# Blockwise causal attention followed by a maxout MLP on one core: the loads and pieces of the opening stage in another order

## The chip, the core and the metric

The kernel runs on one core of one Trainium2 chip. The metric is the device time of one execution in microseconds, as the median of several runs. Engines are named as in the profile: PE (TensorE matmul), PEld (its weight loads), DVE (VectorE), ACT (ScalarE), POOL (GpSimd) and SP (SyncE, which here only issues transfers).

## The reference

Attention over 8 batches of 8 heads, 576 rows, head dimension 64, with a causal mask by blocks of 64; its output, laid out as 4608 tokens by 512, goes through an MLP whose hidden layer is the larger of two products. All inputs and the output are float32.

```python
scores = (1 / sqrt(64)) * q @ k.T              # per batch and head, 576 x 576
scores = where(row // 64 >= col // 64, scores, -1e9)
attn = softmax(scores) @ v
x = attn.transpose(0, 2, 1, 3).reshape(4608, 512)
h1, h2 = x @ w1, x @ w2                        # w1, w2: 512 x 1024
out = maximum(h1, h2) @ w_out                  # w_out: 1024 x 512
```

## The kernel before

**Work and units.** Two heads make a pair (32 pairs, four in each batch), two pairs a group (16 groups, numbered from 0; group g holds pairs 2g and 2g+1; groups 0 and 1 are batch 0, groups 2 and 3 batch 1). The MLP is rewritten with max(h1, h2) = h2 + max(h1 - h2, 0): `diff_w(j)` (line 183, on DVE) forms block j of `d_sb` = w1 - w2 out of the float32 block `w1raw` and the bfloat16 block of w2; there are four blocks of 256 columns. `m_unit` (line 249) forms `m_sb` = w2 @ w_out once. Then `h_unit(i, f)` (line 226) is four matmuls of 128x512 and a max with 0 on DVE (line 231), for the span i of 512 tokens and the slice f of 128 hidden columns: f = 0, 1 need block 0 of `d_sb`, f = 2, 3 block 1, f = 4, 5 block 2, f = 6, 7 block 3. `y_unit` (line 268) is twelve matmuls, a copy (273) and a store (274) for 128 tokens.

**The order is written out by hand.** There is no scheduler: each engine does its instructions in the order in which the program states them. MLP units stand in one list, and `fill(n)` puts the next n matmuls of that list (a matmul of `m_unit` counts a half) between pieces of attention, as far as the tokens they need are finished (`done_tokens`). So PE always has something in the program between two pieces of attention, but what it has there is fixed when the program is written.

**Attention of a group.** `load_qk(g, ..., gated=True)` puts a one-element memset of the raw buffer on POOL (line 114) and then a request for 576 KB of q and one for 576 KB of k on SP's queue (line 115); the memset holds SP back until POOL has come to that place. `cast` (155) turns the float32 rows into bfloat16, `transposes` (357) are 18 small matmuls for q and 18 for k, each into two PSUM buffers, which are copied out (365) by the two engines named in the call. `tile_0`, `tile_1`, `tile_2` compute scores (376, 394), ACT takes their exponential (400, 458), POOL zeroes the masked corners (`mask`, 405) and pads keys (`pad_keys`, 383). `av` (486) multiplies with V and normalizes on DVE (492, 493). `x_out` (524 to 530) transposes a group's result into `xT`, which frees tokens for the MLP; from group 4 on a transfer does this.

**Buffers and queues that matter here.** `ps_m` has four PSUM buffers in rotation; the outputs of `m_unit`, `h_unit`, `y_unit`, `transposes`, `av` and `x_out` all use them, so a matmul that begins a new buffer waits until the buffer's former content was read. `ps_s` has two, for scores. Requests for q and k go through SP's queue; those for V (`load_v`, five chunks for each batch), for w1 (`load_w1`, four blocks of 512 KB), w2 and w_out through POOL's, in the order of POOL's program.

**The opening stage.** Groups 0 and 1 (pairs 0 to 3) are written out call by call, then groups 2 and 3 of batch 1 up to the loop `for g in range(GPB + 1, NG)` (GPB = 2). In the loop, group g's first two score tiles come first, then for each of its pairs p a `fill`, `av_with(p - LAG, ...)` for the pair two before, the next group's `transposes`, two score tiles, and `pool_work(p)`, which issues the loads and casts of later groups. `pool_work(4)` and `pool_work(5)` are called ahead of the loop.

Of the kernel before, what the change touches and what calls it, by code (L numbers as in the profile page):

```python
# [14 lines left out]
def kernel(  # L15
# [91 lines left out]
    def load_qk(g, queues, gated=False):  # L107
        b, u = divmod(g, GPB)
        for nm, src, queue in (("q", q, queues[0]), ("k", k, queues[1])):
            if queue is None or by_dma(nm, g):  # L110
                continue
            raws[nm, g] = t = raw.tile([P, 2, RPP * D], FP32, name=f"{nm}raw")
            if gated:
                nc.gpsimd.memset(t[:, 0, :1], 0.0)
            queue.dma_start(
                out=t[:],
                in_=src[b, 4 * u:4 * u + 4].rearrange(
                    "(s h) (p t) d -> (h p) s (t d)", h=2, t=RPP),
            )
# [4 lines left out]
    def by_dma(nm, g):  # L124
        return g >= T_DMA.get(nm, NG)

    def load_blocks(nm, g):
        b, u = divmod(g, GPB)
        blk_n[nm, g] = n = raw.tile([P, S // BLK, 2, D], BF16, name=f"{nm}b", tag=f"{nm}raw")
        for h in range(2):  # L130
            for s in range(2):
                nc.gpsimd.dma_start(  # L132
                    out=n[h * BLK:(h + 1) * BLK, :, s],
                    in_=(q if nm == "q" else k)[b, 4 * u + 2 * s + h].rearrange(
                        "(j p) d -> p j d", p=BLK),
                )
# [10 lines left out]
    def cast(nm, g, parts):  # L147
        if by_dma(nm, g):
            return
        t = raws[nm, g].rearrange("p s (t d) -> p t s d", d=D)  # L150
        if (nm, g) not in qk_n:
            qk_n[nm, g] = qkn.tile([P, RPP, 2, D], BF16, name=f"{nm}n")
        n = qk_n[nm, g]
        for copy, j0, j1 in parts:
            copy(out=n[:, j0:j1], in_=t[:, j0:j1])  # L155

    def load_v(b, c):
        rows = min(P, S - c * P)
        nc.gpsimd.dma_start(  # L159
            out=vv_r[b % NV][P - rows:, c, :, :D],  # L160
            in_=v[b, :, c * P:c * P + rows, :].rearrange("h p d -> p h d"),
        )
# [12 lines left out]
    def load_w1(j):  # L175
        w1_raw[j] = wraw.tile([P, NDM, WB], FP32, name="w1raw")
        nc.gpsimd.dma_start(out=w1_raw[j][:], in_=w1r[:, :, j * WB:(j + 1) * WB])
# [149 lines left out]
    def fill(n):  # L327
        while n > 0:
            if not current:
                k = next((k for k, t in enumerate(todo) if t[2] <= done_tokens[0]), None)  # L330
                if k is None:
                    return max(0, n)
                current.append(todo.pop(k))
            t = current[0]
            next(t[1])
            n -= t[3]
            t[0] -= 1
            if not t[0]:
                current.pop()
        return 0  # L340
# [10 lines left out]
    def transposes(nm, g, copies):  # L351
        n = qk_n.pop((nm, g))
        pts = [ps_m.tile([P, RPP, NP], BF16, name=f"ps_{nm}T", tag="m") for _ in range(2)]
        for j in range(RPP):
            for i in range(2):
                r = slice(i * NP, (i + 1) * NP)
                nc.tensor.transpose(  # L357
                    pts[i][:, j, :], n[r, j].rearrange("p s d -> p (s d)"), ident[r, r],
                )

        def copy_out(which=(0, 1), part=(0, NP), copy=None):
            p0, p1 = part
            for i in which:
                t = (qT_r if nm == "q" else kT_r)[(2 * g + i) % NT]
                (copy or copies[i])(  # L365
                    out=t[:, p0 * RPP:p1 * RPP].rearrange("q (p j) -> q p j", j=RPP),
                    in_=pts[i][:, :, p0:p1].rearrange("q j p -> q p j"),
                )
        return copy_out
# [69 lines left out]
    def tile_0(p):  # L439
        u = ps_s.tile([P, 2, 512], FP32, name="ps_s", tag="s")  # L440
        scores(p, u, 0, 0, 0, 512)
        return lambda: (exp(p, u, 512, 0), mask(p, 0))

    def tile_1(p):
        u = ps_s.tile([P, 2, 512], FP32, name="ps_s", tag="s")
        scores(p, u, 0, 0, 512, 64)
        scores(p, u, 64, 1, 128, 448)
        return lambda: (exp(p, u, 512, 512), mask(p, 576))

    def tile_2(p):  # L450
        u = ps_s.tile([P, 2, 512], FP32, name="ps_s", tag="s")
        corner_scores(p, u, 320)
        scores(p, u, 0, 2, 256, 320)
        scores(p, u, 384, 3, 448, P)

        def out():
            exp(p, u, 512, 1024)
            nc.scalar.activation(  # L458
                out=aT_r[p % NA][BLK:, :, 1536:AW], in_=u[BLK:, :, 320:320 + BLK],
                func=AF.Exp, scale=scale,  # L460
            )
            mask(p, 1024)
            mask(p, 1344)
        return out

    def region(*tiles):
        for out in tiles:
            out()
# [29 lines left out]
    def x_by_dma(g):  # L498
        return BY_DMA <= g < NG - 1
# [47 lines left out]

    def pool_work(s):
        g, i = divmod(s, 2)
        if s == 4:  # L550
            load_qk(4, (SP, SP), gated=True)
        elif s == 5:
            load_qk(5, (SP, SP), gated=True)
            cast("q", 4, ((pool, 0, RPP),))
            cast("k", 4, ((pool, 0, RPP),))
        else:
            if i == 1 and g + 3 < NG:
                load_qk(g + 3, (SP, SP), gated=True)
            if i == 1 and g + 2 < NG:
                cast("q", g + 2, ((pool, 0, RPP),))  # L560
                cast("k", g + 2, ((pool, 0, RPP),))
            nb, j = divmod(s + 2, HP)
            if nb < B:
                for c in ((0, 1), (2, 3), (4,), ())[j]:
                    load_v(nb, c)
            for nm in "qk":
                if i == 1 and g + 3 < NG and by_dma(nm, g + 3):
                    load_blocks(nm, g + 3)

    T_AT = {s: [("qk"[s % 2], s // 2 + 1)] for s in range(NPAIR - 2)}  # L570
    T_AT[0] = T_AT[1] = T_AT[2] = T_AT[3] = []
# [62 lines left out]
    burst_q3(2)  # L634
    masks_q(2)
    load_w1(1)
    load_w1(2)
    fill(2)
    burst_q1(3)
    fill(2)  # L640
# [2 lines left out]
    av(2, [2, 3, 4])  # L643
    burst_q3(3)
    masks_q(3)
    load_w1(3)
    cast("q", 2, ((pool, 0, RPP),))
    load_qk(3, (SP, SP), gated=True)
    cast("k", 2, ((pool, 0, RPP),))
    load_v(1, 0)  # L650
    fill(8)
    av(3, [2, 3, 4])
    fill(4)
    x_out(1, 0, NCH, (act, act))
    fill(4)
    transposes("q", 2, (dve, act))()
    transposes("k", 2, (dve, act))()
    pad_keys(4)
    pad_keys(5)
# [1 line left out]
    diff_w(0)  # L661
    fill(4)
    region(tile_0(4), tile_1(4))
    load_v(1, 2)
    load_v(1, 3)
    fill(8)
    region(tile_2(4), tile_0(5))
    load_v(1, 4)
    diff_w(1)
    fill(8)  # L670
    region(tile_1(5), tile_2(5))
    diff_w(2)
    cast("q", 3, ((pool, 0, RPP),))
    cast("k", 3, ((pool, 0, RPP),))
    fill(4)
    diff_w(3)
    n = fill_of(GPB)
    fill(n // 2)
    transposes("q", 3, (dve, act))()
    pool_work(4)  # L680
    fill(n // 3)
    transposes("k", 3, (dve, act))()
    pad_keys(6)
    pad_keys(7)
    pool_work(5)
    fill(n - n // 2 - n // 3)

    for g in range(GPB + 1, NG):
        a, b = 2 * g, 2 * g + 1
        old = done_tokens[0]  # L690
        if x_due:
            x_out(x_due.pop())
        n, new = fill_of(g), done_tokens[0]
        region(tile_0(a), tile_1(a))
        lo, hi = max(3, n // 18), n * 2 // 9
        for p, tiles in ((a, lambda: (tile_2(a), tile_0(b))), (b, lambda: (tile_1(b), tile_2(b)))):
            done_tokens[0] = old if p == a and x_by_dma(g - 2) else new
            fill(hi)
            av_with(p - LAG, lo)
            done_tokens[0] = new  # L700
            if p % 2 and x_by_dma(g - 1):
                x_dma(g - 1)
            if p % 2 == 0:
                for nm in "qk":
                    if g + 1 < NG and by_dma(nm, g + 1):
                        transpose_blocks(nm, g + 1)
            copy_out = t_pair(p)
            outs = tiles()
            copy_out()
            region(*outs)  # L710
            if p % 2 and g + 1 < NG:
                pad_keys(p + 1)
                pad_keys(p + 2)
            pool_work(p)
        x_due.append(g - 1)
        fill(n - 2 * (lo + hi))
    for p in range(NPAIR - LAG, NPAIR):
        if x_due:
            x_out(x_due.pop())
        av_with(p, 5)  # L720
        if p % 2 and x_by_dma(p // 2):
            x_dma(p // 2)
        fill(9)
# [42 lines left out]
```

## Time and profile before

| | us |
|---|---|
| median of 3 runs (258.1 to 258.43) | 258.12 |
| the profiled execution's own time | 258.55 |
| its span, first to last instruction | 256.8 |
| PE busy | 245.8 (96%) |
| DVE, ACT, POOL busy | 149.6, 119.6, 122.8 |
| mean granted TensorE clock | 0.997 |

The page lists each engine's busy time, 40 slices of the span, the chain of work that ended last, and groups of instructions; single answers of the trace (waits, timelines, transfers, busy time by stretch) are read for one part of the span. A time such as 28.92 is in microseconds from the first instruction. The end of a matmul is modelled, so PE's busy share says where it is idle, not how well it is used.

### The profile page before, as it was taken

To read this page: it belongs to the slowest core of one execution; us is meant where nothing else is said; L and a number is where in the kernel's file an instruction comes from. 1 tells how busy PE (TensorE), PEld (TensorE's weight loads), DVE (VectorE), ACT (ScalarE), POOL (GpSimd) and SP (SyncE) were. 2 spreads that over 40 slices of the span, in tenths; PEclk is the share of its full clock that TensorE was granted. 3 is DMA by queue.
4 is the path that set the end of the run, shared out by engine and by line. 5 is a ranking of instruction groups with operands and counts; after the bars stand their busy time and mean duration, and the time that the engine had idled before them with its cause. 6 is when DMAs were issued, how large, how long until landed. Compare 5 with 4: busy or idle time off the path is not lost.

```text
span 256.8 us, 6746 instructions
## 1 busy us (share of the span) xinstructions
PE 245.8 (96%) x2768; PEld 132.8 (52%) x2768; DVE 149.6 (58%) x300; ACT 119.6 (47%) x159; POOL 122.8 (48%) x289
## 2 busy tenths in 40 slices
PE   8899898988999999999999999999999999999994
PEld 2467553645555555555555555455545564444443
DVE  4987569557476457545753575357635754753521
ACT  2876492778555555556464646464646300000000
POOL 1984565589768556855675568547231100000000
PEclk9999999999999999999999999999999999999998
DMA  7999999889999999999999999999961312111222
GB/s 247 213 156 249 342 313 131 304 80 214 193 152 201 156 213 157 215 159 219 159 208 151 219 161 201 148 225 154 112 140 59 79 43 83 41 43 41 80 84 83
DMA packets 104383, 41.27 MB, mean 161 GB/s; under 512 B 89248, under 2 KB 93728, under 8 KB 104352
## 3 DMA queue, kind: packets, MB, share of 16 engines
q0 software_dynamic: 65952, 11.87, 61.6%
q1 hardware_dynamic: 37984, 28.32, 46.3%
q10 hardware_dynamic: 416, 0.66, 0.7%
q8 instruction: 21, 0.34, 0.6%
q14 instruction: 10, 0.08, 0.1%
HBM read 34.60 MB, written 9.44 MB: 172 GB/s over the span
## 4 chain that ended last, share of the span: by engine, by line
PE 81%; POOL 6%; DMA 6%; ACT 3%; issue 2%; DVE 1%; POOLq 0%
PE ps_y L268 34%; PE ps_h L226 23%; PE ps_o L486 9%; PE ps_s L376 7%; DMA wo_sb<-in_moe_w_out_dram 4%; PE ps_w L346 2%; DMA vv<-in_v_dram 2%; PE ps_qT L357 2%; ACT aT L400 2%; PE ps_M L249 2%; POOL kb L132 1%; POOL xT L180 1%; POOL qn L155 1%; PE ps_y L283 1%; POOL aT L405 1%
## 5 line engine op out<-in xcount | busy, mean ns | idle before, releaser
L400 ACT ACTIVATE aT<-ps_s 128x1024 bf16<-128x1024 f32 (+2 forms) x100 | 95.8, 994 | 43.7 <-PE ps_s L376 32.9
L268 PE MATMUL ps_y<-wo_sb,g 128*128 128x512 bf16 x280 | 71.1, 380 | 0.0
L226 PE MATMUL ps_h<-xT,d_sb 128*128 128x512 bf16 x288 | 67.9, 380 | 0.0
L231 DVE TENSOR_SCALAR g<-ps_h 128x512 bf16<-128x512 f32 x72 | 49.6, 690 | 19.0 <-PE ps_h L226 18.9
L405 POOL MEMSET aT<- 64x128 bf16 x128 | 23.1, 201 | 66.2 <-ACT aT L400 65.4
L273 DVE COPY y<-ps_y 128x512 f32<-128x512 f32 x35 | 24.2, 692 | 45.5 <-PE ps_y L268 44.7
L486 PEld LDWEIGHTS <-aT 128*128 128x128 bf16 x960 | 37.5, 98 | 14.6 <-issue 1.2
L226 PEld LDWEIGHTS <-d_sb 128*128 128x128 bf16 x288 | 26.5, 98 | 31.2 <-issue 2.6
L268 PEld LDWEIGHTS <-g 128*128 128x128 bf16 x280 | 24.7, 98 | 30.3 <-issue 5.7
L486 PE MATMUL ps_o<-vv,aT 128*128 128x65 bf16 x960 | 39.9, 194 | 0.4 <-DMA vv<-in_v_dram 0.4
L268 PE MATMUL ps_y<-m_sb,xT 128*128 128x512 bf16 x140 | 38.4, 379 | 0.0
L159 POOL DMA_DIRECT2D vv<-in_v_dram x40 | 34.0, 855 | 0.9 <-issue 0.5
L376 PE MATMUL ps_s<-qT,kT 64*128 64x128 bf16 (+6 forms) x344 | 31.6, 281 | 2.6 <-ACT aT L458 1.5
L493 DVE TENSOR_TENSOR xp<-ps_o,rec 128x256 bf16<-128x256 f32 (+1 forms) x64 | 31.4, 490 | 2.2
L132 POOL DMA_DIRECT2D kb<-in_k_dram x40 | 29.4, 760 | 0.0
L492 DVE RECIPROCAL rec<-ps_o 128x4 f32<-128x4 f32 (+1 forms) x64 | 11.9, 186 | 23.7 <-PE ps_o L486 23.4
L288 ACT COPY y<-ps_y 128x256 f32<-128x256 f32 (+1 forms) x2 | 0.6, 320 | 49.3 <-PE ps_y L283 49.3
L365 ACT COPY qT<-ps_qT 128x576 bf16<-128x576 bf16 x15 | 9.6, 640 | 26.9 <-PE ps_qT L357 26.9
L155 POOL CAST qn<-qraw 128x1152 bf16<-128x1152 f32 (+1 forms) x15 | 17.1, 1141 | 7.1 <-DMA qraw<-in_q_dram 6.0
L268 PEld LDWEIGHTS <-xT 128*128 128x128 bf16 x140 | 12.8, 98 | 13.5 <-issue 0.5
L376 PEld LDWEIGHTS <-kT 64*128 64x128 bf16 x344 | 11.8, 94 | 14.2 <-issue 9.0
L365 DVE COPY qT<-ps_qT 128x576 bf16<-128x576 bf16 x17 | 12.7, 749 | 0.7 <-PE ps_qT L357 0.7
(58 smaller groups left out, 135.7 us busy)
## 6 DMA issues: line engine op xcount, KB each, us to landing
qraw<-in_q_dram SPq DMA_DIRECT2D x16, 576.0 KB, 4.6
out_dram<-y SPq DMA_DIRECT2D x35, 256.0 KB, 3.4
vv<-in_v_dram POOLq DMA_DIRECT2D x32, 128.0 KB, 5.5
kraw<-in_k_dram SPq DMA_DIRECT2D x5, 576.0 KB, 7.6
kb<-in_k_dram POOLq DMA_DIRECT2D x40, 72.0 KB, 6.5
w1raw<-in_moe_w_dram POOLq DMA_DIRECT2D x4, 512.0 KB, 13.9
xT<-in_moe_w_dram POOLq DMA_DIRECT2D x4, 256.0 KB, 6.2
wo_sb<-in_moe_w_out_dram POOLq DMA_DIRECT2D x2, 512.0 KB, 10.9
```

Source lines behind the costliest of these rows:

```text
L132: nc.gpsimd.dma_start(out=n[h * BLK:(h + 1) * BLK, :, s], in_=(q if nm == "q" else k)[b, 4 * u + 2 * s + h].rearrange("(j p) d -> p j d", ...
L159: nc.gpsimd.dma_start(out=vv_r[b % NV][P - rows:, c, :, :D], in_=v[b, :, c * P:c * P + rows, :].rearrange("h p d -> p h d"),)
L226: nc.tensor.matmul(pt[:], d_sb[:, c, f * P:(f + 1) * P], xT[:, c, t0:t0 + SPAN], start=(c == 0), stop=(c == NDM - 1),)
L231: nc.vector.tensor_scalar_max(g[:, f], pt[:], 0.0)
L268: nc.tensor.matmul(py[:], lhs, rhs, start=(n == 0), stop=(n == len(terms) - 1),)
L273: nc.vector.tensor_copy(out=y[:], in_=py[:])
L365: (copy or copies[i])(out=t[:, p0 * RPP:p1 * RPP].rearrange("q (p j) -> q p j", j=RPP), in_=pts[i][:, :, p0:p1].rearrange("q j p -> q p j"),)
L376: nc.tensor.matmul(ps[:, hh, col:col + w], kT[r, k0:k0 + P], qT[r, q0:q0 + w], start=True, stop=True,)
L400: nc.scalar.activation(out=aT_r[p % NA][:, :, a0:a0 + w], in_=ps[:, :, :w], func=AF.Exp, scale=scale,)
L405: (eng or nc.gpsimd).memset(aT_r[p % NA][BLK:, :, a0:a0 + BLK], 0.0)
L486: nc.tensor.matmul(po[:, gi, hh, :], a[:, hh, a0:a0 + P], vv[:, c, h0 + 2 * hh, :], start=(mm == 0), stop=(mm == n_mm - 1),)
L493: nc.vector.tensor_mul(xp[:, :, ts[0]:ts[0] + n, p % 2].rearrange("q s t d -> q t s d"), po[:, :, :, :D], rec[:, :n].to_broadcast([P, n, 2 ...
```

## The change

In the opening stage the requests, casts and fillers stand elsewhere; in the loop group 3 and 4 differ. Nothing is computed differently, and PE has the same number of matmuls.

- Group 3's q and k are requested directly behind the masks of pair 3, ahead of group 2's casts. Blocks 2 and 3 of w1 are requested later, between chunks of V.
- q of group 3 is cast on POOL right after the first two score tiles of pair 4; k of group 3 is cast on DVE, behind `diff_w(1)`. The transposes of group 3 stand before and behind the last two score tiles of pair 5; those of k are copied out by DVE alone.
- Groups 4 and 5 are requested at earlier places of the program; their special cases in `pool_work` go.
- `diff_w(2)` and `diff_w(3)` come later relative to the hidden units, and there are fewer fillers ahead of the loop (28 matmuls of `h_unit` before, 17 after, ahead of the scores of pair 6).
- `av` of pairs 6 and 7 comes half a group sooner, and `x_out(3)` with it.

```diff
     def pool_work(s):
         g, i = divmod(s, 2)
-        if s == 4:
-            load_qk(4, (SP, SP), gated=True)
-        elif s == 5:
-            load_qk(5, (SP, SP), gated=True)
-            cast("q", 4, ((pool, 0, RPP),))
-            cast("k", 4, ((pool, 0, RPP),))
-        else:
-            if i == 1 and g + 3 < NG:
-                load_qk(g + 3, (SP, SP), gated=True)
...
+        if i == 1 and g + 3 < NG:
+            load_qk(g + 3, (SP, SP), gated=True)
...
     masks_q(2)
     load_w1(1)
-    load_w1(2)
     fill(2)
...
     masks_q(3)
-    load_w1(3)
+    load_qk(3, (SP, SP), gated=True)
     cast("q", 2, ((pool, 0, RPP),))
-    load_qk(3, (SP, SP), gated=True)
     cast("k", 2, ((pool, 0, RPP),))
     load_v(1, 0)
+    load_w1(2)
     fill(8)
     av(3, [2, 3, 4])
     fill(4)
     x_out(1, 0, NCH, (act, act))
     fill(4)
     transposes("q", 2, (dve, act))()
+    fill(5)
     transposes("k", 2, (dve, act))()
     pad_keys(4)
     pad_keys(5)
     load_v(1, 1)
     diff_w(0)
     fill(4)
     region(tile_0(4), tile_1(4))
+    cast("q", 3, ((pool, 0, RPP),))
     load_v(1, 2)
-    load_v(1, 3)
+    load_w1(3)
+    load_qk(4, (SP, SP), gated=True)
+    diff_w(1)
+    cast("k", 3, ((dve, 0, RPP),))
     fill(8)
     region(tile_2(4), tile_0(5))
+    load_v(1, 3)
     load_v(1, 4)
-    diff_w(1)
     fill(8)
-    region(tile_1(5), tile_2(5))
+    copy_out = transposes("q", 3, (dve, act))
+    outs = tile_1(5), tile_2(5)
+    copy_out()
+    region(*outs)
+    fill(4)
     diff_w(2)
-    cast("q", 3, ((pool, 0, RPP),))
-    cast("k", 3, ((pool, 0, RPP),))
-    fill(4)
-    diff_w(3)
-    n = fill_of(GPB)
-    fill(n // 2)
-    transposes("q", 3, (dve, act))()
-    pool_work(4)
-    fill(n // 3)
-    transposes("k", 3, (dve, act))()
+    transposes("k", 3, (dve, dve))()
     pad_keys(6)
     pad_keys(7)
-    pool_work(5)
-    fill(n - n // 2 - n // 3)
+    load_qk(5, (SP, SP), gated=True)
+    cast("q", 4, ((pool, 0, RPP),))
+    cast("k", 4, ((pool, 0, RPP),))
+    fill(4)

     for g in range(GPB + 1, NG):
...
+            if p == 6:
+                diff_w(3)
             fill(hi)
-            av_with(p - LAG, lo)
+            if p == 9:
+                x_out(3)
+                new = done_tokens[0]
+            else:
+                av_with(p - 1 if p == 8 else p - LAG, lo)
...
-        x_due.append(g - 1)
+        if g != GPB + 2:
+            x_due.append(g - 1)
         fill(n - 2 * (lo + hi))
+        if g == GPB + 1:
+            av_with(6, lo)
```

More of the change, by code (lines that the diff above doesn't have):

```diff
@@ L549, in pool_work @@
         g, i = divmod(s, 2)
-        if s == 4:
-            load_qk(4, (SP, SP), gated=True)
-        elif s == 5:
-            load_qk(5, (SP, SP), gated=True)
-            cast("q", 4, ((pool, 0, RPP),))
-            cast("k", 4, ((pool, 0, RPP),))
-        else:
-            if i == 1 and g + 3 < NG:
-                load_qk(g + 3, (SP, SP), gated=True)
[L559 to L568, printed above, removed]
+        if i == 1 and g + 3 < NG:
+            load_qk(g + 3, (SP, SP), gated=True)
+        if i == 1 and g + 2 < NG:
+            cast("q", g + 2, ((pool, 0, RPP),))
+            cast("k", g + 2, ((pool, 0, RPP),))
+        nb, j = divmod(s + 2, HP)
+        if nb < B:
+            for c in ((0, 1), (2, 3), (4,), ())[j]:
+                load_v(nb, c)
+        for nm in "qk":
+            if i == 1 and g + 3 < NG and by_dma(nm, g + 3):
+                load_blocks(nm, g + 3)
     T_AT = {s: [("qk"[s % 2], s // 2 + 1)] for s in range(NPAIR - 2)}
```

## The prediction

> **What bounds the kernel now.** I read the page's busy times and slices first, to see which engine fills the span and where it does not.
>
> ```profile
> PE 245.8 (96%) x2768; PEld 132.8 (52%) x2768; DVE 149.6 (58%) x300; ACT 119.6 (47%) x159; POOL 122.8 (48%) x289
> ...
> PE   8899898988999999999999999999999999999994
> ```
>
> PE bounds it. From the eleventh slice (70 us) on it is never idle until 252.9. The order of PE's program differs only between the transposes of group 2's k (about 29 us) and about 87 us; ahead of and behind that it is instruction for instruction the same, and the matmuls are the same in number. So the time can change only by PE's idle time in between. Second, the busy time of the stretch 28 to 70, and who made PE wait in it (columns: total, times, longest):
>
> ```profile
> 28.00:70.00 42.00, 37.84 (x567) 21.55 (x565) 26.72 (x49) 28.83 (x42) 30.45 (x66) 1.00 1.21 222
> ```
>
> ```profile
> PE ps_s L376 <- ACT aT L458: 1.5, 2, 0.8
> PE ps_kT L357 <- POOL kn L155: 1.2, 1, 1.2
> PE ps_qT L357 <- POOL qn L155: 0.8, 1, 0.8
> PE ps_o L486 <- DMA vv<-in_v_dram: 0.4, 1, 0.4
> ```
>
> The idle time is 42 - 37.84 = 4.16 us: the most that the change can bring (1.6%). Third, timelines of PE, POOL, SP and DVE, for the places:
>
> ```profile
> 30.12 0.44 PE L357 MATMUL ps_kT<-ident,kn 64*128 64x64 bf16 x18 [1.20 <-POOL kn L155]
> ...
> 41.13 0.44 PE L357 MATMUL ps_qT<-ident,qn 64*128 64x64 bf16 x18 [0.76 <-POOL qn L155]
> ...
> 44.42 0.61 PE L376 MATMUL ps_s<-qT,kT 64*128 64x512 bf16 x6
> ```
>
> ```profile
> 39.34 1.74 POOL L155 CAST qn<-qraw 128x1152 bf16<-128x1152 f32 x1
> ```
>
> ```profile
> 27.88 0.41 SPq L115 DMA_DIRECT2D kraw<-in_k_dram  x1
> ```
>
> ```profile
> 33.78 1.23 DVE L183 TENSOR_TENSOR d_sb<-w1raw,xT 128x1024 bf16<-128x1024 f32 x1 [0.66 <-DMA w1raw<-in_moe_w_dram]
> ```
>
> The row at 44.42 is the scores of pair 6; by then PE has done 28 matmuls of the hidden layer. Last, the transfers between 32 and 34 us (packets, MB, share of the engines):
>
> ```profile
> q0 software_dynamic: 120, 0.44, 61.1%
> q1 hardware_dynamic: 122, 0.28, 42.0%
> ```
>
> POOL's queue (q0) and SP's (q1) share the engines packet for packet; together they move 350 to 366 GB/s in the stretches from 28 to 36.
>
> [...] the q cast at 39.34 stood behind masks though q had landed at 36.9. [...] that cast took 1.74 us beside a subtraction on DVE, casts of the same size without it 1.14.
>
> **The requests.** The masks of pair 3 end at 24.0 on POOL, so k of group 3 is requested at about 24.6 instead of 27.88. Before, it landed 11.8 us after its request, at 39.7. From 28.0, when group 2's k is nearly in, the bytes ahead of its end were four blocks of w1 (2.10 MB), q and k (1.18) and a V chunk (0.13): 3.41 MB at 355 GB/s are 9.6 us, up to 37.6; the last part lagged 2.1 us. Now only two blocks of w1 come first: 2.36 MB, 6.6 us, and the same lag give **36.7** as an estimate (35.3 with two thirds of the lag gone, 37.6 if V's small packets hold it up). But block 1 of w1 now shares with q and k from the start: at 0.28 MB for every 0.44, its 1.05 MB take 4.8 us instead of some 3.6, so it lands at about 34.9 instead of 33.75; block 0 at 32.6 instead of 31.9.
>
> **PE up to q's transposes.** Ten m_unit matmuls (0.98 us for 8 in the chain of waits, so 1.2) fill the wait of 1.20 ahead of k's transposes. They need w_out's second half, which landed at 29.1 (16.42 + 12.7), so they start 0.2 late: gain 1.0. Block 0 of w1 (32.6 + 1.23) costs about 0.2 at the first hidden matmul. Fourteen m_unit matmuls, four score tiles and nine hidden matmuls later PE stands at the transposes of group 3's q at about 36.7.
>
> **The new wait.** The second buffer of these transposes is the one of the first hidden unit, so it needs that unit's max on DVE. In DVE's order the max stands behind diff_w(1) and **behind the cast of k that waits for k's landing**. Diff: 34.9 + 1.22 = 36.1. Cast: starts at 36.75, 1.34 us (group 1's k cast on DVE), 38.0. Max: 0.69 less overlap, 38.65. PE waits 36.7 to 38.7, **2.0 us**, where it waited 0.76. Queued on DVE behind the cast are two maxes, a q copy, diff_w(2), both k copies, diff_w(3). So, on PE: transposes 0.4 (39.1), two score tiles 0.7 (39.8), four hidden matmuls at 0.216 (40.65), k's transposes 0.4 (41.05), three hidden (41.7). The next needs block 2: its max chain (40.6 + 0.65) and diff_w(2) 1.22 end at 42.45, a wait of 0.75; pair 6's scores need the first k copy (0.7): **43.1**. That is 1.3 earlier than 44.42, but only 17 hidden matmuls are done, not 28; the other 11 cost 2.4 later. Break-even is 42.05, so PE is 1.05 us behind.
>
> **Behind that.** DVE still owes a k copy, two maxes and diff_w(3), up to about 46: waits of PE of 0.4 at an av and 0.4 at q's transposes of group 4. V's chunks 3 and 4 of batch 1 are now requested at about 38.3 and 39.2, behind block 3 of w1: they land at 43 with the 3.9 us of a quiet queue, at 47 with the 7.7 of a loaded one, and are needed at 46.5: 0 to 0.6, taken as 0. Of the old waits, the two on ACT (1.5) have about the same causes, with other fillers: 1.1 to 1.5; the V wait (0.44) can go, as batch 2's chunks stand further ahead. Waits behind 44.42 were 1.95 and become about 2.1: +0.15.
>
> **What costs nothing.** Earlier requests for groups 4 and 5 (37.7 instead of 42.23): their casts are not waited for long; covered by PE's fillers. Block 2 is needed at 41.2 and lands near 38.5; block 3, issued behind q's cast and a V chunk near 37, lands at 43 to 44.5 for 44.2 on DVE: 0 to 0.3. POOL loses a cast (1.14); its q cast now stands ahead of a V chunk (0.88 to issue), block 3 (0.75) and pair 4's last masks, up to 2 us late, but pair 4's av needs these only at 46. SP's requests and stores keep their order. Pairs 6 and 7 and x_out(3) half a group sooner change which filler runs on a PE that is never idle there.
>
> **Sum:** +1.05 + 0.15 = +1.2 us. The profiled execution took 258.55 (span 256.8 and 1.75 around it), so it would take 259.75; it stands 0.43 above the median, so against the median of 258.12: **259.3**.
>
> **Rivals.** 0.2%, or 0.5 us, is about what a measurement can tell from no change. (A) Faster: k lands before PE asks. If it is in and diff_w(1) done by 35.1, the wait falls from 2.0 to 0.5 and the sum is -0.3; with the 0.8 on DVE behind it half gone, -0.7: 257.4. For it: the requests are 3.3 us sooner, and the lag of 2.1 us may not return. Against: block 1 must then land as early as before, though it now shares. It decides at k's landing and block 1 both ahead of 35. (B) No change: k at 35.9, +0.3, 258.4: the old waits are exchanged for one on DVE of equal size. (C) Worse: k at 37.6 and V's last chunk after 47: +0.9 and +0.6, 260.8. That the moves do not take effect is no rival: each engine's program has them, with DVE's k cast ahead of the first max.
>
> **How the numbers follow.** The main case 0.55, C 0.15, B 0.17, A 0.13. Slower is the main case and C, 0.70; same B, 0.17; faster A, 0.13. The range goes from 257.7, inside A, to 260.7, just short of C's end, and leaves out some two tenths.
>
> **What would show it.** Right: PE ps_qT waits for DVE g (L231) about 2 us near 38.7; the cast of k on DVE begins when kraw lands, 36 to 37; PE's wait for POOL kn at 30 is gone; pair 6's scores at about 43. Wrong: kraw landed before 35.2 and no such wait (A); or a long wait of ps_o for vv near 47 (C); or PE idle behind 70 us, which no step here foresees.

## The result, and the profile after

The changed kernel takes **266.37 us** (median of 4 runs, 266.01 to 267.24) against 258.11 for the kernel before beside it (257.68 to 258.43): ratio **1.0326, 95% interval 1.0297 to 1.0355**. The forecast was 259.3 with a range up to 260.7: the sign was right, the size was not. The profiled execution took 266.26, with a span of 264.5 against 256.8, so 7.7 us have to be found. The ratios, here and in the experiments, leave out executions more than 1.5% above the fastest of the same kernel.

The page of the changed kernel, its busy times and slices (40 slices of 6.6 us):

```profile
PE 250.2 (95%) x2768; PEld 134.6 (51%) x2768; DVE 151.7 (57%) x302; ACT 119.0 (45%) x158; POOL 122.1 (46%) x288
...
PE   8899698599899999999999999999999999999994
...
PEclk9999979779999999999999999999999999999999
```

The same 2768 matmuls are busy for 4.4 us more (245.8 before), and the row under it says why: the clock granted to PE, which the page of the kernel before has at 9 tenths or more in all slices but the last, falls in the sixth slice (33 to 40 us) and in the eighth and ninth (46 to 60). PE's own row has its holes at or just ahead of those places. The longest waits of PE between 28 and 70 us (in total, times, longest):

```profile
PE ps_o L486 <- DMA vv<-in_v_dram: 2.7, 1, 2.7
PE ps_M L249 <- DMA wo_sb<-in_moe_w_out_dram: 2.2, 1, 2.2
PE ps_h L226 <- DVE d_sb L183: 0.9, 2, 0.6
```

No line of the kernel before is left among the large ones: its waits for POOL's casts are gone, and two transfers have come in their place, a chunk of V and the second half of w_out. The busy time of the same stretch, in the form shown for before (37.84 of 42 there, clock 1.00):

```profile
28.00:70.00 42.00, 35.16 (x483) 19.77 (x483) 25.93 (x46) 23.93 (x35) 25.70 (x54) 0.88 0.99 189
```

The timeline of PE shows where the two waits stand and what the matmuls behind them cost:

```profile
31.56 1.26 PE L249 MATMUL ps_M<-wo_sb,bT_sb 128*128 128x256 bf16 x10 [2.19 <-DMA wo_sb<-in_moe_w_out_dram]
...
45.26 1.25 PE L226 MATMUL ps_h<-xT,d_sb 128*128 128x512 bf16 x5
...
51.17 0.98 PE L486 MATMUL ps_o<-vv,aT 128*128 128x65 bf16 x15 [2.70 <-DMA vv<-in_v_dram]
...
53.59 2.31 PE L226 MATMUL ps_h<-xT,d_sb 128*128 128x512 bf16 x5
```

Five hidden matmuls take 2.31 us at 53.59, where five take 1.25 at 45.26, ahead of the second wait. PE's busy time and granted clock in fine stretches (the second and third figure, then the clock):

```profile
32.80:33.00 0.20, 0.20 (x15) 0.78 1.12 401
33.00:33.20 0.20, 0.20 (x14) 0.50 1.00 366
...
36.20:36.40 0.20, 0.20 (x3) 0.69 0.47 184
```

```profile
49.80:50.20 0.40, 0.00 (x0) 0.72 0.99 282
50.20:50.60 0.40, 0.00 (x0) 0.50 1.07 259
...
56.60:57.00 0.40, 0.40 (x3) 0.74 0.00 0
```

The clock is at half from 32.95 to 36.3, and from 50.0 to 56.8. PE worked for 3.36 us of the first stretch and 5.63 of the second (51.17 to 56.8), and did half the work in them: 1.7 and 2.8 us lost, **4.5** together, which is the 4.4 more of busy time. The rest is idle time: 2.68 more between 28 and 70 (37.84 - 35.16), 0.4 more ahead of 28 (25.02 busy before, 24.61 after) and 0.3 behind 70 (180.00 and 179.69 busy of the 180 up to 250). The sum is 7.9, for a span that grew by 7.7.

Why V was late is in the chain of waits of the changed kernel (start, length, what), here with pieces left out:

```profile
38.07 1.14 POOL qn L155
39.21 0.40 POOL vv L159
...
40.02 0.77 POOL w1raw L177
...
41.42 9.70 DMA vv<-in_v_dram
```

The q cast on POOL starts at 38.07, so block 3 of w1 goes out only at 40.02 and V's chunk 3 at 41.42, and this chunk of 128 KB takes 9.70 us. Few bytes moved just ahead of that (the last column is GB/s, the one before it the busy share of the DMA engines, the one before that the clock):

```profile
37.00:38.00 1.00, 1.00 (x9) 0.62 (x7) 1.00 (x2) 1.00 (x3) 0.35 (x2) 1.00 0.93 77
38.00:39.00 1.00, 1.00 (x13) 0.48 (x13) 0.70 (x1) 0.76 (x3) 0.94 (x2) 1.00 1.24 81
39.00:40.00 1.00, 1.00 (x6) 0.49 (x5) 0.56 (x1) 0.95 (x3) 1.00 (x2) 1.00 0.17 26
40.00:41.00 1.00, 1.00 (x28) 0.45 (x27) 0.83 (x3) 0.98 (x2) 0.94 (x5) 1.00 0.15 10
```

From 37 to 41 at most 81 GB/s moved. Until shortly before 39 the engines were still busy, with the small packets of one chunk of V (nearly all of the 1033 packets from 37 to 39 are under 512 bytes, 0.16 MB in all); from 39 to 41 they were all but idle. Then block 3 (landed 46.06), group 4's q and k (46.98, 49.37) and V's last chunks (51.12, 51.61) were all asked for between 40.0 and 42.3. Before, block 3 was requested at 24.04 and landed at 38.36, and V's chunks 3 and 4 were in at 44.4 and 44.8.

### The profile page after: what moved, and what is told of

It is laid out like the page before. It is cut to its first block, busy times and chain, and to the rows that moved or that the text cites. A ratio compares the mean times of both kernels' runs of the same rounds, so it can differ in the third digit from the quotient of the medians.

```text
span 264.5 us, 6753 instructions
## 1 busy us (share of the span) xinstructions
PE 250.2 (95%) x2768; PEld 134.6 (51%) x2768; DVE 151.7 (57%) x302; ACT 119.0 (45%) x158; POOL 122.1 (46%) x288
## 4 chain that ended last, share of the span: by engine, by line
PE 80%; DMA 13%; POOL 3%; ACT 1%; issue 1%; DVE 0%; ACTq 0%; POOLq 0%
PE ps_y L268 35%; PE ps_h L226 22%; PE ps_o L486 10%; PE ps_s L376 7%; DMA vv<-in_v_dram 6%; DMA wo_sb<-in_moe_w_out_dram 5%; DMA qraw<-in_q_dram 2%; PE ps_qT L357 2%; POOL vv L159 1%; PE ps_M L249 1%; PE ps_y L283 1%; ACT aT L400 1%; PE ps_s L394 1%; POOL qn L155 1%; PE ps_kT L357 0%
## 5 line engine op out<-in xcount | busy, mean ns | idle before, releaser
L226 PE MATMUL ps_h<-xT,d_sb 128*128 128x512 bf16 x288 | 70.1, 385 | 0.9 <-DVE d_sb L183 0.9
L273 DVE COPY y<-ps_y 128x512 f32<-128x512 f32 x35 | 24.2, 691 | 48.8 <-PE ps_y L268 48.2
L486 PE MATMUL ps_o<-vv,aT 128*128 128x65 bf16 x960 | 40.6, 195 | 3.5 <-DMA vv<-in_v_dram 3.3
L268 PEld LDWEIGHTS <-g 128*128 128x128 bf16 x280 | 24.9, 98 | 30.6 <-issue 5.4
L268 PE MATMUL ps_y<-m_sb,xT 128*128 128x512 bf16 x140 | 38.3, 379 | 0.0
L376 PE MATMUL ps_s<-qT,kT 64*128 64x128 bf16 (+6 forms) x344 | 32.3, 286 | 1.6 <-ACT kT L365 0.7
L365 ACT COPY qT<-ps_qT 128x576 bf16<-128x576 bf16 x15 | 9.6, 639 | 28.5 <-PE ps_qT L357 27.2
```

Of the source, the lines that this page charges most:

```text
L226: nc.tensor.matmul(pt[:], d_sb[:, c, f * P:(f + 1) * P], xT[:, c, t0:t0 + SPAN], start=(c == 0), stop=(c == NDM - 1),)
L268: nc.tensor.matmul(py[:], lhs, rhs, start=(n == 0), stop=(n == len(terms) - 1),)
L273: nc.vector.tensor_copy(out=y[:], in_=py[:])
L365: (copy or copies[i])(out=t[:, p0 * RPP:p1 * RPP].rearrange("q (p j) -> q p j", j=RPP), in_=pts[i][:, :, p0:p1].rearrange("q j p -> q p j"),)
L376: nc.tensor.matmul(ps[:, hh, col:col + w], kT[r, k0:k0 + P], qT[r, q0:q0 + w], start=True, stop=True,)
L486: nc.tensor.matmul(po[:, gi, hh, :], a[:, hh, a0:a0 + P], vv[:, c, h0 + 2 * hh, :], start=(mm == 0), stop=(mm == n_mm - 1),)
```

## The experiments

The theory after the result: two transfers come over 2 us late, PE stands for them, and **each time the half clock that follows costs about as much again**; block 3 of w1 and V late in POOL's queue make the larger part, the early request of group 3's q and k the smaller. The rivals: PE's new order with its waits for DVE costs the time; V is held up by group 4's q and k alone; the loop part costs something; idle times cost their own length and no more.

The experiments ran in three groups on three chips (e1 to e4; e5 to e8; e9, e10, g1 and g2), each group with the kernel before beside it, which scatters more there (medians 258.6 to 258.8, single executions 257.4 to 264.1). So ratios to it are compared, not medians, and a step such as that from e3 to e5 joins two chips.

### One part undone: group 3's request (e3_q3_old)

```diff
     masks_q(3)
-    load_qk(3, (SP, SP), gated=True)
     cast("q", 2, ((pool, 0, RPP),))
+    load_qk(3, (SP, SP), gated=True)
```

> The changed kernel with group 3's q, k requested behind group 2's q cast, as in the kernel before. Theory: w_out's second half and k of group 2 land about 2 us sooner, so the wait of 2.2 us at 29.4 and the half clock behind it (1.9 us) shrink to some 0.5; k of group 3 lands near 38 and DVE's cast of it then holds the maxes back, so that a wait of 1.5 to 2.5 us appears at the transposes of group 3's q: 263 to 266. Rival (the early request is no part of the loss): 266 or more, with the wait at 29.4 unchanged.

Measured: ratio 1.0284 (1.0208 to 1.036). w_out's second half landed at 29.42, and PE's wait for it fell to 0.26 with the clock at 1.00 from 28 to 36. But the timeline of PE then has

```profile
49.49 0.65 PE L486 MATMUL ps_o<-vv,aT 128*128 128x65 bf16 x9 [2.37 <-DMA vv<-in_v_dram]
```

Block 3 was issued at 38.44 and V's chunk 3 landed at 49.45 instead of 51.12, and the span is 1.7 shorter (262.8). So the first stall is cured, but the 1.9 us that PE no longer stands there it stands at three other places: 0.64 for the cast of group 2's k, 0.74 for the first hidden unit's max, and 0.84 instead of 0.31 for block 3's difference. What is gained in this trace is the half clock behind the first stall, 1.7 us; the stall for V is nearly as long as before and the clock is at half from 48.2 to 55.0 behind it. The ratio alone would not tell e3 from the changed kernel (1.0326), as the intervals overlap.

### V ahead of block 3 (e2_v_first)

```diff
     load_v(1, 2)
+    load_v(1, 3)
+    load_v(1, 4)
     load_w1(3)
     load_qk(4, (SP, SP), gated=True)
...
     region(tile_2(4), tile_0(5))
-    load_v(1, 3)
-    load_v(1, 4)
```

> The changed kernel with V's chunks 3 and 4 requested ahead of block 3 of w1 and of group 4's q, k. Theory: they land before PE asks, so the wait of 2.7 us near 48.5 and the half clock behind it (about 2.7 us lost) go; block 3 of w1 lands up to 1.8 later and its subtraction is waited for 1 to 1.8 us longer: 262 to 263. Rival (V is late for any order, because all transfers of this stretch are): no gain, 266.

Measured: ratio 1.0184 (1.0094 to 1.0273), four executions from 262.15 to 267.38. PE's waits in the traced execution, of 267.11 (no trace shows those of 262.15 and 264.66, on which the ratio rests):

```profile
PE ps_h L226 <- DVE d_sb L183: 5.5, 2, 4.9
PE ps_M L249 <- DMA wo_sb<-in_moe_w_out_dram: 3.6, 2, 3.1
```

V's chunk 3 now lands at 47.57 and isn't waited for, but block 3, issued at 43.45, lands at 51.30, and PE stands 4.9 us for the difference formed out of it. In this execution the lateness only moved from V to block 3; the wait for w_out was longer too (3.1).

### Block 3 forward, then V as well (e5_w3_early, e6_all_early)

e5, on top of e3's edit:

```diff
     load_w1(2)
+    load_w1(3)
     fill(8)
...
     load_v(1, 2)
-    load_w1(3)
     load_qk(4, (SP, SP), gated=True)
```

e6, on top of e5:

```diff
     load_v(1, 2)
+    load_v(1, 3)
+    load_v(1, 4)
     load_qk(4, (SP, SP), gated=True)
...
     region(tile_2(4), tile_0(5))
-    load_v(1, 3)
-    load_v(1, 4)
```

> The changed kernel with two of its moves undone: group 3's q, k are requested behind group 2's q cast again, and block 3 of w1 right behind block 2 instead of behind group 3's q cast. V's chunks 3, 4 and group 4's requests stay as changed. Theory (what costs the 8 us is PE standing over 2 us for two late transfers, w_out's second half and V's chunk 3, and the half clock that follows each time; V is late because block 3's 1.05 MB is issued only at 40 and stands ahead of it in POOL's queue beside group 4's q, k): block 3 lands at about 40, V's chunk 3 by 46.5, PE's longest wait is under 1 us, the granted clock stays 1.00, 258.5 to 260. Rival 1 (group 4's q, k alone hold V's small packets up): V's chunk 3 lands at 48 to 50 though block 3 is out of the way, and the time stays above 262. Rival 2 (the loss lies in PE's order, with its waits for the maxes on DVE): both transfers in time and still above 262.

> As e5_w3_early, and V's chunks 3, 4 of batch 1 are issued right behind chunk 2, ahead of group 4's requests. Theory: no transfer is late any more; V's chunks land by 44, no wait for them, clock 1.00, 258 to 259.5, what is left over the kernel before being the waits for maxes and differences on DVE that were forecast (about 1). Rival 1: as much better than e5_w3_early as V's wait there was long, else the same. Rival 2 (PE's order): above 262.

Measured: e5 ratio **1.0072** (1.0042 to 1.0103), e6 **1.0032** (1.0006 to 1.0059). Block 3 alone (512 KB; the 1.05 MB of the first expectation are two blocks) brings the ratio from 1.0284 to 1.0072, about 5.5 us: it lands at 39.4 instead of 44.7 in e3. V's chunk 3 lands at 45.98, in time for the 46.5 expected. But the last chunk, asked for at 39.38 behind group 4's q and k (38.02), landed at 47.88 and was waited for 1.47, with a wait of 0.46 for V ahead of it, and the clock was at half from 48.9 to 52.3 behind the two, so the expected 1.00 and "under 1 us" did not come. In e6 this chunk lands 2.8 us sooner, at 45.07: it is asked for 1.35 sooner and takes 1.46 less. So standing beside group 4's q and k can explain only part of the step from e5 to e6, which is about 1 us, and the two intervals overlap. In e6's trace the clock is 1.00 until PE's last matmul. What is left there, in its timeline of PE:

```profile
38.60 0.42 PE L357 MATMUL ps_qT<-ident,qn 64*128 64x64 bf16 x17 [1.16 <-DVE g L231]
...
42.16 0.39 PE L226 MATMUL ps_h<-xT,d_sb 128*128 128x512 bf16 x1 [0.58 <-DVE d_sb L183]
42.82 0.61 PE L376 MATMUL ps_s<-qT,kT 64*128 64x512 bf16 x6 [0.28 <-DVE kT L365]
```

These are the waits that the prediction had worked out: 2.0 for the first hidden unit's max behind the cast of k, 0.75 for block 2's difference, pair 6's scores at 43.1. The trace also has 0.87 at 47.57 for the cast of group 4's q, and 1.50 at 24.65 for w_out's first half, whose landing scatters (last section). PE's new order, as a rival for the loss, is worth 0.8 us (0.06 to 0.59%), not 8.

### The request of group 3 by itself (e7_q3_only, e9_q3_early)

e7 is the kernel before with this edit; e9 is e6 with group 3's request ahead of the q cast again.

```diff
     masks_q(3)
+    load_qk(3, (SP, SP), gated=True)
     load_w1(3)
     cast("q", 2, ((pool, 0, RPP),))
-    load_qk(3, (SP, SP), gated=True)
```

> The kernel before with one edit: group 3's q, k are requested behind pair 3's masks, ahead of block 3 of w1 and of group 2's q cast; all else as before. Theory: 1.18 MB more shares the engines with w_out's second half and group 2's k, so that w_out's last part lands 1 to 2 us later (31 instead of 29.1) and PE waits 1 to 2 us for it ahead of or behind group 2's k transposes; with less than 2 us of it in one piece the clock stays 1.00: 258.5 to 260. If the wait is over 2 us and the clock halves behind it, 261 to 262. Rival (the lateness of w_out in the changed kernel was a chance of that execution or came from the later blocks of w1): w_out at 29 to 29.5 as before, 257.5 to 258.3.

> As e6_all_early, but group 3's q, k are requested where the changed kernel has them, ahead of group 2's q cast; so it is the changed kernel with block 3 of w1 and V's chunks 3, 4 alone brought forward. Theory: w_out's last part at 31 to 32.5 again, PE waits over 2 us for it and has half the clock for some 3.4 us behind that, as in e7_q3_only; V in time, no second stall: 2 to 3.5 us more than e6_all_early, 261 to 263. Rival (the early request costs only where the three later blocks of w1 stand behind w_out as well, as in e7_q3_only): the same as e6_all_early, 259 to 260.

Measured: e7 ratio 1.0115 (1.0048 to 1.0182); e9 1.0078 (1.0037 to 1.012), 0.5% above e6 with overlapping intervals. The landing of w_out's second half over all traces falls into two groups:

| group 3's q requested | w_out's second half landed |
|---|---|
| as changed, 24.0 to 24.9 (after, e1, e2, e7, e9) | 31.51, 31.21, 32.32, 32.68, 32.98: mean 32.1 |
| as before, 27.2 to 28.0 (before, e3 to e6, e8, e10, the two with gaps) | 29.14 to 30.49: mean 29.7 |

So the early request makes that landing 2.5 us later, every time. Its price is less sure. In e9 PE waited 1.34 for it and kept its clock, in e7 it did not wait for it at all. The half clock in both traces follows a wait for the **first** half, which landed at 25.72 in e7 and 24.70 in e9. That half is not made late by the early request: it landed at 24.4 in the mean of the five traces with it and at 24.5 in the mean of the nine without, late also where nothing ahead of it was changed (last section). The timeline of PE in e7 and its clock, then the timeline in e9, where the clock is at half from 25.0 to 28.4:

```profile
25.77 2.98 PE L249 MATMUL ps_M<-wo_sb,bT_sb 128*128 128x256 bf16 x16 [2.22 <-DMA wo_sb<-in_moe_w_out_dram]
```

```profile
27.00:28.00 1.00, 1.00 (x7) 0.50 1.34 244
```

```profile
24.74 3.35 PE L249 MATMUL ps_M<-wo_sb,bT_sb 128*128 128x256 bf16 x16 [1.76 <-DMA wo_sb<-in_moe_w_out_dram]
```

So the waits forecast for the second half (1 to 2 us in e7, over 2 us and the half clock in e9) did not come in that size, and four runs don't tell how much of e7's 3 us is the edit's. Between e6 and e9 it is 1.2 us at the centre, and not told apart from nothing. Why exactly w_out's second half is held up was not tried by itself.

### The loop part alone (e4_loop_only)

The kernel before with the change's edits to the loop (pairs 6 and 7's values and `x_out(3)` half a group sooner), without the move of `diff_w(3)`.

```diff
-            av_with(p - LAG, lo)
+            if p == 9:
+                x_out(3)
+                new = done_tokens[0]
+            else:
+                av_with(p - 1 if p == 8 else p - LAG, lo)
...
+        if g == GPB + 1:
+            av_with(6, lo)
```

> The kernel before with the loop's part of the change alone: av of pairs 6 and 7 and x_out(3) half a group sooner. Theory: other fillers on a PE that is never idle there, 258.1 within 0.5. Rival (the loop's part costs): 260 or more.

Measured: ratio 1.0025 (0.9995 to 1.0055), span 256.3 in the profiled execution. Not told apart from nothing; at most 0.6%.

### The clock: dummies in the gaps, and gaps by themselves (e1_warm, g1_gap_short, g2_gap_long)

e1 gives PE matmuls on zeros where it would stand:

```diff
     transposes("q", 2, (dve, act))()
+    warm_up(10)
     fill(5)
...
         fill(n)
+        if p == 4:
+            warm_up(12)
         av(p, [2, 3, 4])
```

> The changed kernel with dummy matmuls that keep PE at work in its two long waits: ten of 128x512 ahead of the fillers behind q's transposes of group 2 (2.2 us), twelve ahead of pair 4's second av (2.6 us); nothing is left out. Theory (two late landings, and an idle PE loses half its clock for some 4 to 6 us afterwards): the waits themselves stay, filled with dummies, but the clock stays at 1.00, so 1.9 + 2.7 = 4.6 us come back: about 261.8. Rival (the clock falls for another reason, or the lost time lies in the loop): 266 or, with 4.8 us of added matmuls that do not all fit into the waits, more.

Measured: ratio 1.0239 (1.0134 to 1.0344), so the 261.8 of the theory was not reached. The ten dummies kept the clock at 1.00 from 28 to 36, though w_out landed late (31.21). The twelve did not do it at the second place: PE waited 1.62 for a difference just ahead of them, then 1.62 for V behind them, and the clock was 0.82 from 52 to 54 and 0.50 from 54 to 56. Two of the other executions had a mean clock of 1.000 and took 263.35 and 263.87; the traced one took 266.78. So e1 bears the theory out at the first place only. The gaps measure it away from everything else, in the last 45 us of the kernel before (`gate` is a tile of zeros that nothing else uses):

```diff
+    def gap(n):
+        pw = ps_m.tile([P, SPAN], FP32, name="ps_w", tag="m")
+        nc.tensor.matmul(pw[:], gate[:], zeros[:], start=True, stop=True)
+        for _ in range(n):
+            nc.gpsimd.memset(gate[:], 0.0)
+        nc.tensor.matmul(pw[:], gate[:], zeros[:], start=True, stop=True)
...
+    for _ in range(5):
+        fill(36)
+        gap(5)                  # g1; gap(11) in g2
     fill(len(units) * NFF * 12)
```

> The kernel before with five idle times of PE added in its last 45 us, where PE is otherwise never idle and POOL has nothing to do: behind every 36 units of filler a matmul that reads a tile (128x128), five memsets of that tile by POOL, a matmul that reads it again. The ten matmuls add 2.2 us. Each idle time is estimated at about 1.2 us. Theory (idle times of 1.2 do not move the clock): the clock stays 1.00, the time grows by 2.2 and the five idle times, about 8, to 266. Rival (any idle time brings the clock down): over 270.

> As g1_gap_short with eleven memsets each: idle times of about 2.5 us. Theory (an idle time over 2 us is followed by half the clock for about 3.4 us or a multiple of it): the clock falls to 0.50 behind most of the five, each costs 1.7 us or more beyond its own idle time, together 6 to 12 more than 2.2 and the idle times: with 12.5 idle, 279 to 285. Rival (an idle time costs itself and no more; the half clock in the changed kernel came from elsewhere): 273, clock 1.00.

Measured: g1 267.15 (ratio 1.0311, 1.0263 to 1.0359), g2 281.07 (1.0858, 1.079 to 1.0925). PE's waits for the gate, g1 first, then g2. Four of the five gaps lie between matmuls of the MLP; the fifth stands behind the last of them, beside the closing copy and store:

```profile
PE ps_w L594 <- POOL gate L593: 5.7, 4, 1.4
```

```profile
PE ps_w L594 <- POOL gate L593: 12.0, 4, 3.0
```

Four idle times of 1.43 and the eight matmuls of 0.216 around them make 7.5; behind the last matmul of the MLP g1 goes on for 4.1 us where the kernel before takes 3.8. The sum is 7.8; g1 is 8.5 above the kernel before (6.8 to 9.3 by the interval) and its clock stays at 1.00 to PE's end: idle times of 1.43 us cost themselves here. In g2 the same sum is 12.0, 1.7 and 1.9 (5.7 instead of 3.8), together 15.6; g2 is 22.4 above, 6.8 more. The clock in g2 behind its second and third gap:

```profile
243.00:247.00 4.00, 3.91 (x11) 0.58 0.03 10
247.00:252.00 5.00, 5.00 (x25) 0.99 0.12 44
252.00:257.00 5.00, 2.00 (x10) 1.00 0.14 52
257.00:261.00 4.00, 3.81 (x11) 0.57 0.00 0
```

It is at half from 243.7 to 247.1 and from 257.3 to 260.7, 3.4 us each with PE at work in it, so 1.7 us are lost each time, 3.4 of the 6.8. The rest is not the gaps' alone: the traced execution, of 283.04, also had a stall and half clock in its opening (last section), and where the other three (279.18, 279.29, 282.84) lost theirs no trace shows. Behind the first and fourth gap, as long, the clock stays at 1.00. The theory as written ("an idle time over 2 us is followed by the half clock") is therefore too simple; what the traces show of it is told in the last section.

### The wait of before filled (e8_fill_only, e10_fill_cast)

e8 is the kernel before with the change's `fill(5)` between group 2's q and k transposes. e10 adds:

```diff
     fill(8)
+    cast("q", 3, ((pool, 0, RPP),))
     region(tile_1(5), tile_2(5))
     diff_w(2)
-    cast("q", 3, ((pool, 0, RPP),))
     cast("k", 3, ((pool, 0, RPP),))
```

> The kernel before with one edit: fill(5), ten m_unit matmuls, between group 2's q and k transposes, into PE's wait of 1.20 us. Theory: the wait goes from 1.20 to 0 or 0.2, and as PE waits for hardly anything that it would not wait for otherwise behind it, 0.7 to 1.1 us are gained: 257.0 to 257.4, ratio 0.996 to 0.997. Rival (PE comes to a later wait the sooner: for w1's first blocks' differences near 34 and for q at 41): 257.8 to 258.2, the 1.2 us reappear as waits for d_sb or qn.

> As e8_fill_only (ten m_unit matmuls between group 2's transposes), and group 3's q cast on POOL ahead of the last masks of pair 5 instead of behind them. Theory: q lands at 37, the cast runs at about 37.8 to 39 instead of 39.3 to 41.1, so that PE's wait of 0.8 us at the transposes of group 3's q goes, and the masks, 1.2 us later, are not waited for: 0.5 to 0.8 better than e8_fill_only, ratio to before 0.993 to 0.996. Rival (PE, earlier at these transposes, waits for the next thing, the k cast or d's last blocks on DVE): the same as e8_fill_only, 0.997.

Measured: e8 0.9972 (0.9943 to 1.0001), e10 0.9979 (0.9947 to 1.001). The wait of 1.20 is gone in both, the centre of e8 is the 0.7 us that it should bring, and both intervals still hold 1. In e10 the wait of 0.8 for the q cast left as well, and two others came in the same place; its waits there:

```profile
PE ps_qT L357 <- DVE g L231: 0.6, 1, 0.6
...
PE ps_s L376 <- DVE kT L365: 0.3, 1, 0.3
```

That is the rival's forecast in the time and in the engine, though PE waits for a max and a copy and not for the cast or the differences. So of all that the change does, only the ten fillers may be worth keeping; no version here is shown to beat the kernel before.

## Why the prediction was wrong

By its own steps:

- **"What costs nothing ... block 3, issued behind q's cast and a V chunk near 37, lands at 43 to 44.5", and V's chunks "requested at about 38.3 and 39.2 ... 0 to 0.6, taken as 0".** This is the step that failed by most. Block 3 was issued at 40.02 and V's chunks at 41.42 and 42.30, since POOL's timeline has ahead of them, in the program's order, two masks that waited 0.41 and 0.65 us for ACT, the q cast (1.14 us from 38.07) and a V chunk's issue (0.88 from 39.15). Each issue was priced, but not what its lateness brings together: the DMA engines were all but idle from 39 to 41, and then block 3, group 4's q and k and V's last chunks shared the engines. Chunk 3 took 9.70 us where 7.7 was the top of the estimate, and was 4.6 later than the 46.5 at which it was to be needed. That top was too low by the trace of the kernel before itself, where the five chunks of batch 1 took 10.5, 10.2, 9.3, 9.3 and 7.7. In part the lateness came from the first stall, but e3, without that stall, still has V at 49.45. Price, the half clock with it: about 5.5 us for block 3 (e3 to e5), about 1 for V's last chunks (e5 to e6).
- **"They need w_out's second half, which landed at 29.1, so they start 0.2 late: gain 1.0."** Failed. The sharing with the early q and k was charged to w1's blocks and to k, not to w_out, which was in POOL's queue at the same time. It landed at 31.51; the wait of 1.20 became one of 2.19. The same edit without the early request (e8) shows a gain of about the right size, 0.7 at the centre of an interval that just holds none. How much of the loss the early request makes is not settled (e3, e9).
- **The clock was in no step.** Every idle time was priced at its length. Of the 7.7 us, 4.5 are half clock (0.50 behind the waits of 2.19 and 2.70). That, and a lateness of 4.6 instead of some 0.6, is why rival C, which named the right place ("V's last chunk after 47"), stopped at 260.8.
- **"The new wait": right in its mechanism, and hidden in the changed kernel.** So the sign of the forecast came true for a reason that did not decide this time, which is luck. There PE came to q3's transposes behind the first stall, when k's cast was done (it ended at 38.7; the first max began at 39.44, waiting for PE). With the stalls taken away (e6) the wait is 1.16 instead of 2.0, the one for block 2 0.58 instead of 0.75, and pair 6's scores start at 42.82 instead of 43.1. The remaining loss of e6, 0.8 us, stands against the forecast of 1.2 for the whole change; e6 lacks its early request.
- **The requests.** k of group 3 landed at 35.91 (forecast 36.7), block 1 of w1 at 36.19 (34.9), block 0 at 33.80 (32.6): the early q and k gain a little more, and what they share the engines with loses 1.2 to 1.3 more than was charged. k came as early as rival B asked (35.9), and it decided nothing, since PE stood elsewhere.
- **"The loop part costs nothing":** e4, 1.0025 with 1 inside its interval, agrees.
- **"PE idle behind 70 us"** hardly came (0.3 us).
- **A reading.** The q cast at 39.34, which stood behind masks with q landed at 36.9, is POOL's, so it shows POOL's order. That DVE keeps the program's order too, on which "The new wait" rests, was not shown by it; e6's trace shows it for this place: the first hidden unit's four matmuls are the first of a row that starts at 35.40, and its max began only at 37.86, behind the k cast (1.35 us from 36.59), which had waited 1.61 for k.

## What to carry to other kernels

Look at the granted clock as soon as a change can make PE stand for about 2 us: here each of the two cost nearly as much again or as much again in half clock (2.19 and 1.7, 2.70 and 2.8), so a forecast must not price it at its length alone. When requests are moved, list all that is in flight or still to be requested on every queue, not just the tile that the change is about: here a load pushed behind a cast and masks on the issuing engine left the DMA engines idle first and crowded afterwards (busy share 0.17 and 0.15 from 39 to 41, 0.96 to 1.59 in the three stretches of 2 us from 42 to 48). And a stall taken away ahead of a transfer that is still late was largely waited for again at the next places (e3, e2).

## What the runs showed of the hardware

**When the clock halves.** The changes of the clock lie on a grid of about 3.4 us: 32.95, 36.3, 50.0 and 56.8 in the changed kernel are 3.4, 13.7 and 6.8 apart, 1, 4 and 2 times 3.42; 243.7, 247.1, 257.3 and 260.7 in g2 are 3.4, 10.2 and 3.4 apart. Counted over the step of this grid that ends at the fall, PE stood 2.0 us of 3.4 both times in the changed kernel (the second time in three pieces: 0.31, 0.21 and 1.5), 2.8 and 2.2 in g2's second and third gap, 1.9 in e5 (0.46 and 1.47) and 1.76 in e9, in one piece. No fall came with 1.7 in a step (g2's first and fourth gap, each of which the grid, carried on from 243.7 and 260.7, cuts into 1.3 and 1.7) or 1.43 (g1). So for these traces the author's estimate puts the edge between 1.7 and 1.76 of 3.4 us, as far as modelled ends of matmuls can tell; of g2's four gaps of 3.0 two were followed by the half clock and two were not, by where on the grid they fell. The 2 us in one piece, which the expectations took for the edge, is not it (1.76 in e9, and 0.46 and 1.47 in e5, were followed by the half clock). And the step from 50.0 to 53.4 in the changed kernel, in which PE stood for its first 1.2 us, did not bring the clock back, nor did one with 1.5 in e3 (48.2 to 51.6); the next one, without idle time, did both times.

**How much a landing scatters.** In g2, whose program is that of the kernel before up to its last 45 us, w_out's *first* half landed at 26.82 instead of 23.58; PE waited 3.72 for it, and the clock was 0.50 from 25.2 to 32.0. In the other traces it landed between 23.58 and 25.72. PE's wait for that half was at most 1.50 in eleven of the fourteen traces (e6 has the 1.50), and 1.76, 2.22 and 3.72 in e9, e7 and g2, where the half clock followed.
